# A linear recurrence over four batches of eight heads: steps of two batches by four heads, with halves swapped in the second batch

## The chip, the cores and the metric

The kernel runs on one core of a Trainium2 chip. The metric is the device time of one execution in microseconds. It is 399.98 us, the median of 3 runs (399.85 to 400.6).

Engine names are those of the profile: PE (matrix multiply) with PEld (its weight load), DVE (vector), ACT (scalar), POOL (GpSimd) and SP, which issues most DMAs.

## What is computed

A recurrence of the RWKV-5 kind over r, k and v (4 batches, 8 heads, 768 positions, 48 wide, float32), and then a mixture of experts over the 3072 resulting rows of 384:

```
state = zeros((B, H, D, D))
for t in range(S):
    cur = einsum('bhd,bhe->bhde', u * kt, vt)
    y[:, :, t] = einsum('bhd,bhde->bhe', rt, state + cur)
    state = w[:, :, None] * state + einsum('bhd,bhe->bhde', kt, vt)
x = y.transpose(0, 2, 1, 3).reshape(B * S, H * D)
...
# 4 groups x 4 experts; the best group and the best expert in it, a softmax weight of each
h = maximum(x[tokens of e] @ w1[e], 0)          # 384 -> 1024
out[tokens of e] = gate * (h @ w2[e])           # 1024 -> 384
```

## The kernel before

**The recurrence in steps.** Positions are taken 128 at a time. Within such a chunk the recurrence is written with matmuls: scores of keys against queries, masked to earlier positions; the masked scores times v; and the state of the chunks before times the queries. Powers of w are folded into tables: `pw` (multiplied into r when it is turned), `iw` (into the very first k) and `T2` (into the others). There are 24 steps. A step n is one chunk of one batch with all its 8 heads: group g = n // 2 has two batches, and half a = n % 2 picks one. The state of a batch comes back every fourth step (`R[n % 4]`).

**One step** (loop over s, line 860), as it stands on PE:

- `values(s)`: masked scores `am` times v, into bank YB, on two column halves of the array
- `update(s)`: k times v for the state, into bank MS
- `turn(far, ...)`: four transposes each of k (bank TR) and r (bank RW) for a later step
- `rows_out(s - 1)`: four transposes of the result into rows, bank YB
- `gate_sum` and `gate_parts`: the routing logits. gate_parts makes four partial products on four column strips of 32, into a bank of 128 columns, which ACT copies to `lT`; gate_sum adds the strips with the matrix `sel`
- `scores(s + 2)`: for each of four head pairs hc and each e, two matmuls (line 536), on the four quarters of the array: the pair's e picks the rows, and z, the half of the keys, the columns. Keys 0 to 63 meet 128 queries; keys 64 to 127 meet only the last 64, because the others come before them
- `state(s + 1)`: the state times the queries, into YB, on the same four quarters

Beside it DVE masks the scores into `am` (`mask`, line 543, a copy under the predicate `later`), carries the state (`carry`), multiplies `pw` into the turned r and runs the routing (route_1 to route_4). ACT copies results out of PSUM and writes the diagonals of `am` (`diagonal`, line 561; the r*u*k term). POOL multiplies r*k and that by u (`own`, lines 489 and 490), k by T2 (`scaled`, line 493), and scatters finished rows into x_sorted with indirect DMAs (line 230). Order on each engine is the order of the program. In steps 0 to 5 (CLOSE is 5) the scores of step s + 1 are made in step s, so that mask and values follow each other directly; from step 5 on they are made two steps ahead, and the masks one.

**Loads.** r, k and v come in tiles of 128 positions by 2 batches by 8 heads by 48. `load` issues one DMA per batch on SP (line 323). The first r and k are issued on SP and ACT in turn (line 344).

**Start.** POOL and DVE build the tables, PE turns r, k and iw; in between stand transposes whose results aren't used (`turn_nothing`). ACT fills the pads of the k and r tiles, copies u, then T2.

**The end of the recurrence and the experts.** The two largest experts get their first 128 tokens ahead (`up_ahead`, `down_ahead`). Then 16 experts follow in a fixed order; the last one's rows are made token by row (`rows_down`, line 238), multiplied by the gate on ACT (line 244) and scattered by POOL (line 245).

`out_of_range` (line 751) tells whether w lay outside the range that the tables allow; a matmul (line 756) makes its result common to all partitions in step 0.

## Time and profile before

| what | us |
|---|---|
| median of the runs | 399.98 |
| the profiled execution, whole | 402.09 |
| its span, first to last instruction | 400.3 |
| values of step 0, 1, 2, 3 start at | 12.14, 16.86, 20.95, 25.01 |
| values of step 4, 5, 6, 7 start at | 30.57, 37.91, 44.53, 49.53 |
| values of step 23 start at | 127.43 |
| first expert matmul after the recurrence (line 1104) | 152.16 |
| last matmul starts | 392.66 |
| last scatter by POOL starts | 394.03 |

| line | what | count | mean ns |
|---|---|---|---|
| 536 | PE, scores, 128 columns | 368 | 276 |
| 536 | PE, scores, 64 columns | 368 | 235 |
| 583 | PE, values | 384 | 277 |
| 543 | DVE, mask, 128x1024 | 24 | 1323 |
| 561 | ACT, diagonal, 128x128 | 152 | 398 |
| 493 | POOL, k times T2, 128x384 | 24 | 1006 |
| 624 | ACT, lT out of PSUM, 128x128 | 24 | 260 |

The durations of PE are those of single instructions in a pipeline: they overlap, and what a stage costs is read from where it starts and where the next one starts. float32 matmuls show as two instructions each.

### The profile page before, as it was taken

The numbers are of one execution on the slowest core, as the hardware profiler recorded it, in microseconds if no ns is written. First come the engines' busy times: TensorE is split into PE (matmuls) and PEld (weight loads), VectorE is DVE, ScalarE is ACT, GpSimd is POOL, SyncE is SP. The second block draws the span as 40 slices with busy tenths as digits, with TensorE's granted clock in tenths as the row PEclk, the third lists the DMA queues.
The fourth block names the chain that finished last, engine by engine and source line by source line (L and its number), as shares of the span: only waits on it lengthen the run. The fifth ranks groups of instructions, "written<-read, shape, count | busy, mean of one in ns | idle before, by whom it ended". The sixth has DMA issues, their size and how long they took to land.

```text
span 400.3 us, 10467 instructions
## 1 busy us (share of the span) xinstructions
PE 388.7 (97%) x3963; PEld 361.9 (90%) x3963; DVE 153.4 (38%) x405; ACT 180.4 (45%) x429; POOL 201.0 (50%) x265
## 2 busy tenths in 40 slices
PE   8999999999999999999999999999999999999992
PEld 6787899999888977899999999999999999999981
DVE  7887988888867602101202112111121221211110
ACT  4665888888875211432433424424244244244210
POOL 7999956999842412105162351532624524523542
PEclk9999999999999999999999999999999999999999
DMA  8998999995965977999999999999989999981000
GB/s 159 160 174 159 197 208 221 212 195 147 264 200 123 308 193 212 233 275 258 232 258 243 228 250 266 224 253 284 200 240 259 255 247 268 233 236 28 27 18 27
DMA packets 123118, 81.80 MB, mean 204 GB/s; under 512 B 96863, under 2 KB 114289, under 8 KB 123061
## 3 DMA queue, kind: packets, MB, share of 16 engines
q1 hardware_dynamic: 116019, 71.12, 77.1%
q0 software_dynamic: 4752, 9.55, 8.1%
q8 instruction: 32, 0.52, 0.6%
q10 hardware_dynamic: 2290, 0.40, 0.5%
q14 instruction: 25, 0.20, 0.2%
HBM read 69.89 MB, written 11.67 MB: 204 GB/s over the span
## 4 chain that ended last, share of the span: by engine, by line
issue 46%; PE 29%; POOL 18%; SPq 3%; DVE 2%; DMA 1%; POOLq 1%; ACT 0%
POOL out_dram L1128 16%; PE YB L583 6%; PE PA L536 6%; SPq L323 3%; PE TR L511 3%; PE YB L574 2%; PE YB L630 2%; PE RW L511 2%; PE MS L594 2%; PE TR L619 2%; PE MS L644 1%; DMA vt<-in_v_dram 1%; POOL out_dram L245 1%; PE TR L793 1%; DVE am L543 1%
## 5 line engine op out<-in xcount | busy, mean ns | idle before, releaser
L1128 POOL DMA_INDIRECT out_dram<-yt,idn x93 | 90.4, 972 | 137.1 <-DVE yt L1126 107.0
L1076 DVE STREAM_TRANSPOSE xe<-xg 128x672 f32<-128x672 f32 (+2 forms) x16 | 12.7, 796 | 121.0 <-DMA xg<-x_sorted 88.7
L1116 PE MATMUL YB<-hT,w2p 128*128 128x208 f32 (+10 forms) x336 | 58.7, 328 | 0.0
L1116 PE MATMUL PA<-hT,w2p 128*128 128x208 f32 (+10 forms) x336 | 58.1, 326 | 0.0
L1116 PEld LDWEIGHTS YB<-hT,w2p 128*128 128x128 f32 x336 | 55.8, 190 | 0.0
L1116 PEld LDWEIGHTS PA<-hT,w2p 128*128 128x128 f32 x336 | 55.3, 190 | 0.0
L561 ACT ACTIVATE am<-ident,du 128x128 f32<-128x128 f32 x152 | 50.5, 398 | 0.0
L1125 DVE STREAM_TRANSPOSE yt<-yT 128x672 f32<-128x672 f32 (+1 forms) x14 | 11.8, 842 | 80.4 <-ACT yT L1119 80.4
L1094 ACT COPY w2p<-w 128x1024 f32<-128x1024 f32 x42 | 41.1, 1045 | 3.0 <-DMA w<-in_moe_w_dram 3.0
L543 DVE COPY_PREDICATED am<-later,PA 128x1024 f32<-128x1024 int32 x24 | 31.7, 1323 | 10.8 <-PE PA L536 6.1
L1104 PE MATMUL MS<-xe,w 128*128 128x208 f32 (+12 forms) x192 | 32.8, 320 | 0.0
L1104 PE MATMUL TR<-xe,w 128*128 128x208 f32 (+12 forms) x192 | 32.8, 320 | 0.0
L1104 PE MATMUL RW<-xe,w 128*128 128x208 f32 (+12 forms) x192 | 32.8, 320 | 0.0
L1104 PE MATMUL SB<-xe,w 128*128 128x208 f32 (+12 forms) x192 | 32.7, 320 | 0.0
L1104 PEld LDWEIGHTS SB<-xe,w 128*128 128x128 f32 x192 | 30.8, 190 | 0.6 <-issue 0.2
L1104 PEld LDWEIGHTS MS<-xe,w 128*128 128x128 f32 x192 | 30.7, 190 | 0.0
L1104 PEld LDWEIGHTS RW<-xe,w 128*128 128x128 f32 x192 | 30.7, 190 | 0.0
L1104 PEld LDWEIGHTS TR<-xe,w 128*128 128x128 f32 x192 | 30.7, 190 | 0.0
L230 POOL DMA_INDIRECT x_sorted<-xt,place_i x16 | 16.1, 1003 | 23.6 <-DVE end L719 11.8
L536 PE MATMUL PA<-rT,kT 48*64 48x128 f32 (+1 forms) x736 | 25.6, 255 | 0.5 <-issue 0.5
L583 PE MATMUL YB<-am,vt 128*48 128x128 f32 x384 | 25.9, 277 | 0.1
L490 POOL TENSOR_TENSOR dg<-dg,ub 128x384 f32<-128x384 f32 x24 | 24.1, 1003 | 1.9
(220 smaller groups left out, 560.1 us busy)
## 6 DMA issues: line engine op xcount, KB each, us to landing
w<-in_moe_w_dram SPq DMA_DIRECT2D x128, 384.0 KB, 9.5
vt<-in_v_dram SPq DMA_DIRECT2D x24, 192.0 KB, 4.5
rp<-in_r_dram SPq DMA_DIRECT2D x23, 192.0 KB, 4.3
kt<-in_k_dram SPq DMA_DIRECT2D x22, 192.0 KB, 5.2
xg<-x_sorted SPq DMA_DIRECT2D x36, 85.8 KB, 10.3
x_sorted<-zeros SPq DMA_DIRECT2D x4, 392.0 KB, 4.7
out_dram<-yt,idn POOLq DMA_INDIRECT x93, 7.5
xg<-x_sorted SPq DMA_DIRECT2D x20, 73.5 KB, 8.9
```

The source lines that it names most:

```text
L230: ins = nc.gpsimd.indirect_dma_start(out=xs_dram, out_offset=bass.IndirectOffsetOnAxis(ap=place_i[:, i : i + 1], axis=0), in_=xt[:, i].rea ...
L490: nc.gpsimd.tensor_mul(dg, dg, ub)
L511: nc.tensor.transpose(ps[:, hc, :], two, ident)
L536: nc.tensor.matmul(PA[64 * z : 64 * (z + 1), e, P * hc + 64 * z : P * (hc + 1)], lhsT=kT[rows, hc, 64 * z : 64 * (z + 1)], rhs=rT[rows, hc ...
L543: nc.vector.copy_predicated(am[n % NAM], later.unsqueeze(1).unsqueeze(1).to_broadcast([P, 2, HC, P]).bitcast(I32), PA.rearrange("p e (h t) ...
L561: nc.scalar.mul(am[n % NAM][:, e, hc, :], ident, dus[n][:, i : i + 1])
L583: nc.tensor.matmul(y_at(e, hc), lhsT=vt[:, n % 2, 2 * hc + e, :], rhs=amn[:, e, hc, :], start=(n < 4 and hc < 2), stop=True, skip_group_ch ...
L1076: nc.vector.transpose(xe[:, :, 0:nb, :], xg[:, 0:nb, 0:QW].rearrange("p i (ko a) -> p ko i a", a=32))
L1094: nc.scalar.copy(o4[:, kk], v4[:, kk])
L1104: nc.tensor.matmul(ph[:, i, 0:n], lhsT=w1[:, ko, P * (f + i) : P * (f + i + 1)], rhs=xe[:, ko].rearrange("p i b -> p (i b)")[:, 0:n], star ...
L1116: nc.tensor.matmul(po[:, 0:n], lhsT=w2p[:, d, fo, :], rhs=hT[:, fo, 0:n], start=(fo == 0), stop=(fo == FO - 1))
L1128: ins = nc.gpsimd.indirect_dma_start(out=out_q, out_offset=bass.IndirectOffsetOnAxis(ap=idn[:, i : i + 1].bitcast(U32), axis=0), in_=yt[:, ...
```

## The change

A step is now one chunk of two batches with four heads each: step n takes heads 4 (n % 2) to 4 (n % 2) + 3 of both batches of its group. In the second batch of each pair the two halves of a chunk are swapped: partitions 0 to 63 hold positions 64 to 127 and the other way round. So the second batch loads with two DMAs of 64 partitions, its tables PW, IW and T2 are kept a second time with halves swapped, the mask has one triangle per head pair (LT), and token numbers (tok4) follow. In scores the long matmul of the second batch falls to the upper keys: quarters z = 0 and z = 1 exchange their lengths, and the pairs go in the order 0, 2, 1, 3.

gate_parts takes two steps at once (every second step), since a row of the result is now spread over two steps; it writes two blocks of TR, copied at once, and gate_sums has two matmuls. In steps before 5 these stand after the state. In step 4 the values are copied out after the diagonals, and one turn goes to bank PA. The range check moves to step 8 and shares the matmul of a count; fillers in the start go; `rows_of_table(1)` stands after the first scores, with `scaled(0, ...)` behind it. The last expert's rows are made and scattered in two halves of 192.

```diff
-    later = cst([P, P], "later")
+    LT = cst([P, HC, P], "LT")
+    later = LT[:, 0, :]
...
+    def half_down(hT, w2, i, n, z, po, yt):
+        cols = slice(DM // 2 * z, DM // 2 * (z + 1))
+        for fo in range(FO):
+            nc.tensor.matmul(
+                po[0:n, 0 : DM // 2], lhsT=hT[:, fo, 0:n], rhs=w2[:, fo, cols], start=(fo == 0), stop=(fo == FO - 1),
+                skip_group_check=True,
+            )
+        nc.scalar.mul(yt[0:n], po[0:n, 0 : DM // 2], tagA[i][0:n, 1:2])
+        ins = nc.gpsimd.indirect_dma_start(
...
-        def load_half(t, src, g, a, queue):
-            c, b = g // 2, 2 * (g % 2) + a
-            queue.dma_start(out=t[:, a], in_=src[b, :, P * c : P * (c + 1), :].rearrange("h t d -> t h d"))
+        def load_heads(t, src, g, queue, heads=slice(0, H)):
+            for b in range(2):
+                for rows, t0 in ((slice(0, P), 0),) if b == 0 else ((slice(0, 64), 64), (slice(64, P), 0)):
+                    t1 = P * (g // 2) + t0
+                    queue.dma_start(
+                        out=t[rows, b, heads],
+                        in_=src[2 * (g % 2) + b, heads, t1 : t1 + rows.stop - rows.start, :].rearrange("h t d -> t h d"),
+                    )
...
-        for a in range(2):
-            load_half(raw[0, "r"], r, 0, a, both[a])
-            load_half(raw[0, "k"], k, 0, a, both[1 - a])
+        for heads in (slice(0, 4), slice(4, 8)):
+            load_heads(raw[0, "r"], r, 0, nc.sync, heads)
+            load_heads(raw[0, "k"], k, 0, nc.scalar, heads)
...
+        PW = ring.tile([P, 2, HC, P], FP32, name="PW")
+        IW = am[3]
+        pw, iw = PW[:, 0], IW[:, 0]
...
-        turn_nothing(2)
         gates_in()
         pads(kp, 0)
         nc.scalar.copy(ub.rearrange("p h d -> p (h d)"), u_ps_all)
+        for t in (PW, IW):
+            for z in range(2):
+                nc.scalar.copy(t[:, 1, :, 64 * z : 64 * (z + 1)], t[:, 0, :, 64 * (1 - z) : 64 * (2 - z)])
+        for i in (1, 3):
+            nc.scalar.copy(LT[:, i, :], LT[:, i - 1, :])
...
+        def own(g, hf):
+            dg = dgs[2 * g + hf] = pool.tile([P, 2, 4, D], FP32, tag="dg", bufs=3, name="dg")
+            nc.gpsimd.tensor_mul(dg, four(raw[g, "r"], hf), four(raw[g, "k"], hf))
+            nc.gpsimd.tensor_mul(dg, dg, spread(ub[:, 4 * hf : 4 * hf + 4], 1, 2))
+
+        def scaled(g, hf):
+            nc.gpsimd.tensor_mul(four(kp[g % NKP], hf), four(raw[g, "k"], hf), four(T2, hf))
...
+        def columns_of(hc, z):
+            return (64 * z, P) if hc < 2 else (0, 64 * (z + 1))
 
         def scores(n):
             kT, rT = rkT.pop((n, "kT")), rkT[n, "rT"]
-            for hc in range(HC):
+            for hc in (0, 2, 1, 3):
                 for e in range(2):
                     rows = slice(DP * e, DP * e + D)
+                    for z in range(2):
+                        c0, c1 = columns_of(hc, z)
                         nc.tensor.matmul(
+                            PA[64 * z : 64 * (z + 1), e, P * hc + c0 : P * hc + c1],
+                            lhsT=kT[rows, hc, 64 * z : 64 * (z + 1)], rhs=rT[rows, hc, c0:c1],
                             start=True, stop=True, skip_group_check=True,
                         )
...
+        def part(n):
+            for b in range(2):
+                for e in range(2):
+                    q = 2 * (n % 2) + e
+                    nc.tensor.matmul(
+                        TR[32 * q : 32 * (q + 1), b, :], lhsT=gwp[:, 4 * (n % 2) + e, :], rhs=yTs[n][:, e, b, :],
+                        start=True, stop=True, skip_group_check=True,
+                    )
+
+        def gate_parts(n, first=True):
+            if first:
+                part(n - 1)
+            part(n)
+            mid[n] = pool.tile([P, 2, P], FP32, tag="lT", name="lT")
+            nc.scalar.copy(mid[n], TR[:, 0:2, :])
...
+        def rows_of_table(b, ps):
+            for hc in range(HC):
+                nc.tensor.transpose(ps[:, hc, :], IW[:, b, hc], ident)
+            nc.scalar.copy(
+                T2[:, b].rearrange("p (y e) d -> p y e d", e=2),
+                ps.rearrange("p y (e x) -> p y e x", x=DP)[:, :, :, 0:D],
+            )
...
+        rows_of_table(0, RW)
         own(0, 0)
-        scaled(0, 1)
         own(0, 1)
-        scaled(0, 0)
         sum_own(0)
         diagonal_here(0)
         diagonal(0, 1, HERE - HC)
         scores(0)
+        rows_of_table(1, whole_MS)
+        scaled(0, 1)
+        scaled(0, 0)
...
         mask(0)
-        turn_nothing(2)
         turn(1, "rT")
-        turn_nothing(4, TR)
         turn(1, "kT")
...
-            values_out(s)
+            if s != CLOSE - 1:
+                values_out(s)
             if s == 0:
                 own_term(1)
-                out_of_range()
             for n, e, hc in waiting:
                 diagonal(n, e, hc, hc + 1)
             waiting.clear()
+            if s == CLOSE - 1:
+                values_out(s)
...
             if s + 1 < NT:
                 state(s + 1)
+            if s < CLOSE:
+                if summed is not None:
+                    gate_sums(summed)
+                if parts is not None:
+                    gate_parts(parts)
             if s == CLOSE - 1:
-                turn(s + 3, "kT")
+                turn(s + 3, "kT", PA[:, 0].rearrange("p (h t) -> p h t", t=P))
...
+                if p == last:
+                    for z in range(2):
+                        yt = pool.tile([P, DM // 2], FP32, tag="yh", name="yh")
+                        half_down(hTs[p], held(p)[1], 2 + i, SLOTS[i], z, next_of(downs), yt)
```

## The prediction

> **What bounds the kernel now.** I read the page first (busy times and the row of slices), then busy time by stretches of 10 us, then the chain of waits and the timeline of the stages that the change touches.
>
> ```profile
> span 400.3 us, 10467 instructions
> PE 388.7 (97%) x3963; PEld 361.9 (90%) x3963; DVE 153.4 (38%) x405; ACT 180.4 (45%) x429; POOL 201.0 (50%) x265
> ```
>
> ```profile
> 50.00:60.00 10.00, 10.00 (x210) 9.03 (x208) 8.14 (x23) 8.06 (x26) 5.26 (x6) 1.00 0.95 208
> ...
> 70.00:80.00 10.00, 10.00 (x216) 9.06 (x214) 8.06 (x18) 8.05 (x26) 9.49 (x10) 1.00 0.97 212
> ```
>
> Columns: stretch, its length, busy time (and instructions) of PE, PEld, DVE, ACT, POOL, granted clock, DMA share, GB/s. PE is idle between 44 and 393 us only in two stalls of under 0.9 us near 103 and 110, so the experts (from 152 us) cost what their matmuls cost, and the change doesn't touch these. In the recurrence it decides what PE has to do per step. A regular step starts every 4.79 us (values at 59.73 and 64.52):
>
> ```profile
> 62.47 0.30 PE L644 MATMUL MS<-sel,lT 128*128 128x20 f32 x2
> 62.70 0.43 PE L619 MATMUL TR<-yT,gwp 128*32 128x128 f32 x8
> 63.05 0.99 PE L536 MATMUL PA<-rT,kT 48*64 48x128 f32 x30
> 63.78 0.31 PE L574 MATMUL YB<-rT,R 48*48 48x128 f32 x2
> 63.87 0.28 PE L536 MATMUL PA<-rT,kT 48*64 48x128 f32 x2
> 63.92 0.66 PE L574 MATMUL YB<-rT,R 48*48 48x128 f32 x14
> 64.52 0.75 PE L583 MATMUL YB<-am,vt 128*48 128x128 f32 x10
> ```
>
> Start, length, then the group. Two state matmuls (L574) start at 63.78, ahead of two scores matmuls (L536) at 63.87: one half of the array had run out of scores while the other had not. That imbalance is what the swapped halves remove.
>
> Before 44 us PE waits, and the steps are chains through several engines. The start, from the timeline:
>
> ```profile
> 2.43 0.60 ACTq L323 DMA_DIRECT2D rp<-in_r_dram  x1
> 3.06 1.28 ACT L349 ACT_TABLE_LOAD   x1 [3.06 <-DVE pw L380]
> 6.45 1.06 PE L511 MATMUL MS<-ident,rp 128*128 128x128 f32 x4
> 9.25 0.48 ACT L816 COPY T<-YB 128x384 f32<-128x384 f32 x1 [1.18 <-PE YB L815]
> 10.61 0.60 PE L511 MATMUL RW<-ident,rp 128*128 128x128 f32 x4
> 10.76 1.32 DVE L543 COPY_PREDICATED am<-later,PA 128x1024 f32<-128x1024 int32 x1
> 12.14 1.08 PE L583 MATMUL YB<-am,vt 128*48 128x128 f32 x16
> 16.86 1.08 PE L583 MATMUL YB<-am,vt 128*48 128x128 f32 x16
> ```
>
> and step 4 (30.57 to 37.91) from the chain:
>
> ```profile
> 33.13 1.33 DVE am L543
> 34.46 0.24 DVE ts L607
> ...
> 34.84 0.59 PE MS L644 x4
> 35.43 0.40 PE MS L619 x8
> 35.83 0.02 issue
> 35.85 0.27 ACT lT L624
> ```
>
> Mask, carry, logits, copy: DVE, PE and ACT wait in turn.
>
> **What the Trainium skill says.** "TensorEngine Tiling (Array Packing)", Key Properties: tiles load and multiply independently of each other, and a change of tiling mode drains the array. The trace agrees: see the overtaking above; PEld stands idle 0.20 us before the scores and 0.18 before the values, the two changes of mode. "TensorE: Matmul & The Clock Gate", Part 1: after an idle window of about 3.4 us the clock falls to half until a busy window has passed. The trace has only the first warming: four transposes take 1.06 us at 6.45 and 0.60 at 10.61. "DMA: Bandwidth & Descriptors", Anatomy of one DMA: a semaphore wait of a DMA is waited for by the issuing sequencer, with about 2 us fixed from issue to landing. Here ACT loads its table at 3.06, when its last issue ends; a 0.8 KB load took 2.0 us.
>
> **The change part by part.** The sum is made against the profiled execution (402.09 us, span 400.3); it is 2.1 us above the median of 399.98, and differences are carried over to the median unchanged.
>
> *Scores.* Sixteen matmuls in two passes, on four tiles. In the upper tiles a step has 8 passes of 128 columns, in the lower 8 of 64. From the timeline of single groups, passes of 128 follow at 0.109 us in a tile, and passes of 64 at 0.058. Before, the longer tiles take 8 x 0.109 = 0.872 (the chain has 0.92 for the group). After, each tile has 4 x 0.109 + 4 x 0.058 = 0.668. Gain 0.20 to 0.22 a step; the order 0, 2, 1, 3 keeps tiles at most one head apart, a lead that they have in the trace too. I take 0.215. It counts only where PE decides: in steps 6 to 21.
>
> *Gates.* gate_parts for two steps at once uses two column strips per step, four over both; 8 matmuls take 4 passes of 0.109 per strip = 0.44 in place of 0.22, if the second step's strips run beside the first's (if not, 0.7). A gate_sum is 0.22. Even steps: two sums in place of one sum and parts: 0.22 + 0.22 + the change of mode, 0.65, against 0.69 (62.36 to 63.05). Odd steps: parts alone, 0.22 more, and one sum 0.22 less: 0. So a pair of steps gains 2 x 0.215 + 0.04 = 0.47. Pairs 8/9 to 20/21: 7 x 0.47 = 3.3; step 6 gains 0.24; step 7 0.0 (two sums already). Steps 22 and 23 and the head of the tail lose 0.6: a second sum twice, and parts of one step on two strips only (0.22 more each), less one sum. Sum -2.95. The ACT copies (L624, 24 x 0.26) become 12 longer ones; cover: ACT is 0.8 busy. After the speed-up the next limits are POOL, at 4.25 us a step (three multiplies of 1.0 and one scatter) and DVE, 4.06; a PE step averages 4.55, so neither takes over.
>
> *Start.* DMAs: three per load in place of two, with the same bytes and packets; SP issues 25 of them ahead of the gate weights, not 15. In the compiled order a DMA waits for the one eight before it. The last three of ACT's eight loads so wait for the first pieces of r and k; with the first landings at 4.58 and 5.95 now for twice the bytes, I put that at about 4.9, so that ACT's table load starts near 5.4, not 3.06. ACT then also copies four half tables and two masks (4 x 0.31 + 2 x 0.2 = 1.6). T2's first half so comes at about 11.0 (9.73 now), the diagonals end at 12.0 (10.61), mask 0 at 13.3 (12.08). T2's second half ends at 12.4, POOL's scaled(0,1), now ahead of everything on POOL, at 13.4, turn(1,kT) on PE 14.0, and values(0) behind it 14.05 (12.14). Then values, values_out, diagonals, mask: 1.0 + 0.14 + 0.55 + 0.97 + 1.35 = 4.0, so values(1) at 18.05 (16.86; there 0.5 us went to the range matmul L756, which waited for the carry and goes). +1.2. Steps 1 and 2 have ACT's diagonals in this loop (4.06 and 4.09 us now), so shorter scores give nothing. POOL's three more fills and masks (some 0.3 us) lie beside the wait for the tables; its four iotas for one lie behind 1 us of lead.
>
> *Steps 3 to 5.* Step 3: the parts no longer wait for the carry ahead of the state (0.48 idle): -0.55. Step 4: diagonals ahead of values_out bring mask 5 0.7 forward, and the logits stand after the state with turn(7) in another bank; I add up PE alone: 1.0 + 0.75 + 0.5 + 0.6 + 0.95 + 0.7 + 0.5 + 0.7 + 0.95 = 6.6 against 7.34: -0.75. Step 5: the same DVE order up to the carry (4.3 after the start), then sums, scores, state: 6.15 against 6.62: -0.5. Front in all: 1.2 - 1.8 = -0.6.
>
> *Tail.* Last rows in two halves: PE the same 5.2 us, ACT 0.35 for 0.58, but POOL is held by the scatters of the expert before until 392.27 and then needs 1.28 per scatter: the second half issues at 393.9, not 394.03. -0.15. Masks, table multiplies and the memory fills keep their sizes (copy_predicated over 1024 elements 1.32): 0, on DVE with slack. The x_sorted chain after step 23 grows by 0.3; xe is ready 0.85 ahead of PE's need at 152.16, so 0.
>
> Sum: -0.6 - 2.95 - 0.15 = -3.7: span 396.6, median **396.3**.
>
> **Unknown costs.** The parts' overlap: 0 to +0.26 a pair, +2 at most; I take 0, since scores already show such a lead. ACT's wait for lanes: from 0 (table at 3.1, front 2 us better) to 2 us later. The scores' gain: 0 to 0.22. POOL multiplies on two blocks of four heads: rows of 48 out of 64 cost 1010 ns (L489) and contiguous ones 1003 (L490), so 0, at most 0.1 each, still hidden.
>
> **Rivals.** A, the scores don't shorten: 32 weight loads in 0.87 us are 27 ns each, and if loads came one after another, that would be the limit whatever the columns. For: the two numbers coincide. Against: loads of different tiles start 7 ns apart, and state overtakes scores. Time: the 3.4 us of scores gone, 399.7. B, the start is dearer: the idle stretch of PE from about 10.5 to 13.4, with the filler transposes gone, lets the clock fall for one window. Then steps 0 and 1 lose some 2.6 us: 398.9. C, slower: the same fall of the clock, lasting. At half clock the 3.2 us of PE work of a step become 6.4, more than the 4.05 of the loop, 2.3 us a step; because PE is busy only part of these steps the clock may not return. It decides from 3.7 / 2.3, about two steps; with three, 403. Against it: each step has over 3 us of matmuls. That the recurrence is not split as told can be excluded from the compiled order.
>
> **How the numbers follow.** Forecast 0.68 (its own range 394.6 to 397.8), A 0.06, B 0.19, C 0.07. Faster: forecast, B and a part of A, 0.88; within 0.2% (0.8 us, about what this measurement can tell) 0.05, from A; slower 0.07, C. Range 394.3 to 399.0: it holds B's centre and leaves out C, most of A and the edges.
>
> **What would show it.** Values of step 6 near 43.9 (44.53); regular steps alternating near 4.5 and 4.6; no state matmul ahead of a scores matmul; ACT's table load near 5.4; the clock row below 9 early would show B or C. If the step period stays 4.79 the scores' reasoning is wrong; if step 6 starts after 46, the front's.

## The result, and the profile after

The change made the kernel slower: 406.93 us (median of 6 runs, 404.64 to 409.24) against 400.29 for the kernel before in the same series (399.53 to 401.6), a ratio of 1.0158 with an interval of 1.0132 to 1.0184. The profiled execution takes 406.95 us, its span is 405.2, against 402.09 and 400.3 before. The forecast was 396.3 and faster. Some executions of a kernel fall into a slower state, with a lower granted clock; the ratios and intervals below, and the times that are set side by side, leave them out.

The page of the kernel after: its span, the busy times, and the row of granted clocks.

```profile
span 405.2 us, 10586 instructions
PE 386.5 (95%) x3989; PEld 362.1 (89%) x3989; DVE 154.1 (38%) x412; ACT 181.2 (45%) x425; POOL 203.4 (50%) x273
...
PEclk9699999999999999999999999999999999999999
```

PE is busy for 2.2 us less than before (388.7), so its work did shrink; the span grew by 4.9 all the same. The loss is idle time of PE, and the 6 near the left end of the last row (PEclk, tenths of full clock in 40 slices) says that its clock fell once. Laid end to end:

| stretch of the span | before | after | difference | forecast |
|---|---|---|---|---|
| start to values of step 0 | 12.14 | 15.20 | +3.1 | +1.9 |
| step 0 to 1 | 4.72 | 5.09 | +0.4 | -0.7 |
| step 1 to 6 | 27.60 | 27.06 | -0.5 | -1.8 |
| step 6 to 23 | 82.90 | 82.53 | -0.4 | -2.95 with the next row |
| step 23 to the first expert | 24.80 | 25.97 | +1.2 | |
| first expert to the start of the last matmul | 240.50 | 243.67 | +3.2 | 0 |
| from there to the end | 7.64 | 5.68 | -2.0 | -0.15 |

All starts are from the timelines: the values of step 6 at 47.35 (before 44.46; the 44.53 given above is the chain's piece, which begins a little later), of step 23 at 129.88 (127.36), the first expert at 155.85 (152.16).

First, what the change was for. The timeline of PE in a regular step of the kernel after (start, length, group):

```profile
64.84 0.66 PE L673 MATMUL TR<-yT,gwp 128*32 128x128 f32 x16
65.43 0.90 PE L588 MATMUL PA<-rT,kT 48*64 48x128 f32 x32
66.14 0.62 PE L626 MATMUL YB<-rT,R 48*48 48x128 f32 x16
66.69 0.75 PE L638 MATMUL YB<-am,vt 128*48 128x128 f32 x10
```

From the start of the scores (L588) to that of the state (L626) it is 0.71 us, where before it was 0.87 (63.05 to 63.92); no state matmul stands ahead of a scores matmul any more. Undisturbed pairs of steps take 4.46 + 4.68 = 9.14 us, against 9.56. The mechanism of the scores is there, with the forecast size.

Busy time by stretches shows where it goes: the columns are length, PE, PEld, DVE, ACT, POOL, clock, DMA share, GB/s.

```profile
50.00:60.00 10.00, 10.00 (x225) 8.89 (x224) 8.28 (x23) 8.34 (x26) 9.38 (x32) 1.00 0.86 182
...
70.00:80.00 10.00, 8.57 (x199) 7.59 (x199) 7.10 (x17) 6.92 (x21) 9.28 (x10) 1.00 0.93 187
...
200.00:210.00 10.00, 8.89 (x51) 8.57 (x50) 2.91 (x6) 3.79 (x7) 4.46 (x5) 1.00 0.97 257
```

From 70 to 80 PE was full before, and the DMAs moved 212 GB/s; now PE is idle for 1.43 us there, and they move 187. The same from 50 to 60: 182 for 208 GB/s. The timeline names the two stalls in the recurrence (in brackets the idle time and what ended it):

```profile
44.26 0.66 PE L565 MATMUL TR<-ident,kp 128*128 128x128 f32 x4 [1.81 <-POOL kp L538]
...
74.50 0.66 PE L565 MATMUL TR<-ident,kp 128*128 128x128 f32 x4 [1.43 <-POOL kp L538]
```

PE waits for POOL's `kp`, that is for `scaled`. POOL itself is not too slow. Its own timeline:

```profile
34.29 1.01 POOL L534 TENSOR_TENSOR dg<-rp,kt 128x384 f32<-128x384 f32 x1 [3.69 <-DMA rp<-in_r_dram]
...
70.16 1.20 POOL L232 DMA_INDIRECT x_sorted<-xt,place_i  x1 [8.09 <-ACT am L613]
...
73.45 1.00 POOL L538 TENSOR_TENSOR kp<-kt,T 128x384 f32<-128x384 f32 x1
```

At 34.29 POOL has stood idle for 3.69 us until r landed; the work behind it is late by that, and reaches PE at 44.26. Before, at this place, POOL ran without a gap (groups at 32.14, 33.23, 34.55). The second stall has another carrier: POOL is held for 8.09 us ahead of its first scatter of rows into `x_sorted`. The profile puts that down to ACT, but what fits is a DMA: the last of the four fills of `x_sorted` with zeros has to land first (fill_early below tests this). The chain of waits of the kernel after has its issue:

```profile
64.30 0.74 SPq L348
...
65.08 0.65 SPq L480
```

L480 is that fill. An estimate: from 65.08, a landing of 5.3 us (the median of the three fills issued between 20 and 60 us) gives 70.4, and the scatter starts at 70.16. Before, it went out at 57.60, and the timeline of POOL before has

```profile
63.07 1.20 POOL L230 DMA_INDIRECT x_sorted<-xt,place_i  x1 [7.65 <-DVE ohg L178]
```

So the fill is 7.5 us later, though the step in which it belongs is later by only 2.6: SP's queue is behind.

The start, from the timeline of the kernel after:

```profile
6.08 1.28 ACT L376 ACT_TABLE_LOAD   x1 [6.08 <-DMA rp<-in_k_dram]
8.95 0.69 DVE L576 TENSOR_TENSOR rT<-MS,PW 128x512 f32<-128x512 f32 x1 [1.54 <-ACT PW L468]
11.29 0.47 ACT L881 COPY T<-RW 128x384 f32<-128x384 f32 x1
13.09 1.98 POOL L538 TENSOR_TENSOR kp<-rp,T 128x384 f32<-128x384 f32 x2 [1.67 <-ACT T L881]
14.15 1.12 PE L565 MATMUL TR<-ident,kp 128*128 128x128 f32 x4 [1.58 <-POOL kp L538]
15.20 1.95 PE L638 MATMUL YB<-am,vt 128*48 128x128 f32 x16
17.08 1.56 PE L588 MATMUL PA<-rT,kT 48*64 48x128 f32 x32
```

The table load comes at 6.08 (3.06 before), and DVE's first product then waits 1.54 us more for the swapped copy of `PW`, since step 0 now holds both batches. PE has idle gaps of 1.50 us ahead of the first scores at 10.29 and of 1.58 ahead of 14.15. The values take 1.95 us in place of 1.08: the granted clock is 0.50 from 14 to 18 us (it falls between 12.2 and 12.4).

In the experts the page of the kernel after shows, for the issue of the gathers of expert rows (count, KB each, us from issue to landing):

```profile
xg<-x_sorted SPq DMA_DIRECT2D x36, 85.8 KB, 12.6
```

It was 10.3 before. The waits of the kernel after from 125 us on have PE itself waiting for such rows (us in total, number of times, longest):

```profile
PE SB L1187 <- DVE xe L1159: 2.4, 2, 1.3
```

Before, there was no such wait; DVE's `xe` waited for the gathers for 88.7 us in all, now for 149.4.

### The profile page after: what moved, and what is told of

Its sections match the earlier page's. It is cut to its first block, busy times and chain, and to the rows that moved or that the text cites. A ratio compares the mean times of both kernels' runs of the same rounds, so it can differ in the third digit from the quotient of the medians.

```text
span 405.2 us, 10586 instructions
## 1 busy us (share of the span) xinstructions
PE 386.5 (95%) x3989; PEld 362.1 (89%) x3989; DVE 154.1 (38%) x412; ACT 181.2 (45%) x425; POOL 203.4 (50%) x273
## 4 chain that ended last, share of the span: by engine, by line
issue 47%; PE 24%; POOL 20%; DMA 2%; ACT 2%; SPq 2%; DVE 1%; POOLq 1%; ACTq 0%
POOL out_dram L1211 16%; PE YB L638 5%; PE PA L588 4%; PE TR L565 3%; PE YB L626 2%; PE YB L689 2%; PE RW L565 2%; SPq L348 2%; PE TR L673 2%; PE MS L649 2%; DMA kt<-in_k_dram 1%; PE MS L706 1%; DMA rp<-in_k_dram 1%; POOL kp L538 1%; POOL out_dram L247 1%
## 5 line engine op out<-in xcount | busy, mean ns | idle before, releaser
L1159 DVE STREAM_TRANSPOSE xe<-xg 128x672 f32<-128x672 f32 (+2 forms) x16 | 12.7, 797 | 149.4 <-DMA xg<-x_sorted 149.4
L613 ACT ACTIVATE am<-ident,du 128x128 f32<-128x128 f32 x152 | 49.6, 397 | 0.0
L595 DVE COPY_PREDICATED am<-LT,PA 128x1024 f32<-128x1024 int32 x24 | 32.4, 1349 | 9.9 <-ACT am L613 5.1
L1208 DVE STREAM_TRANSPOSE yt<-yT 128x672 f32<-128x672 f32 (+1 forms) x14 | 11.8, 842 | 55.4 <-ACT yT L1202 55.4
L638 PE MATMUL YB<-am,vt 128*48 128x128 f32 x384 | 27.1, 283 | 0.8 <-ACT kT L574 0.5
L638 PEld LDWEIGHTS YB<-am,vt 128*48 128x48 f32 x384 | 20.7, 126 | 5.6 <-issue 4.0
## 6 DMA issues: line engine op xcount, KB each, us to landing
xg<-x_sorted SPq DMA_DIRECT2D x36, 85.8 KB, 12.6
```

The lines of the kernel that those rows point to most:

```text
L595: nc.vector.copy_predicated(am[n % NAM].rearrange("p e h t -> p e (h t)"), spread(LT.rearrange("p h t -> p (h t)"), 1, 2).bitcast(I32), PA,)
L613: nc.scalar.mul(am[n % NAM][:, e, hc, :], ident, dus[n][:, i : i + 1])
L638: nc.tensor.matmul(y_at(e, hc), lhsT=vt[:, *head(n, e, hc), :], rhs=amn[:, e, hc, :], start=(n < 4 and hc < 2), stop=True, skip_group_chec ...
L1159: nc.vector.transpose(xe[:, :, 0:nb, :], xg[:, 0:nb, 0:QW].rearrange("p i (ko a) -> p ko i a", a=32))
```

## The experiments

Theory Q (the queue of loads): the loss comes from the third DMA per load, which puts SP behind, and with it r, the fill and the first data of the experts. Rivals: the start alone does it, by the clock (F) or by the way the first loads are split (S); or the recurrence in two batches by four heads is itself slower, whatever the loads (L in the first two expectations). Later expectations add R: the swapped halves and the shorter scores ask more of POOL, DVE or memory than they give. Each kernel is timed beside the kernel before in the same series.

The first four kernels below (the two without the swap, and the two of the start) ran in a series in which the kernel before took 400.74 us (399.55 to 402.26); all later ones in series in which it took 414 to 424. There the intervals of the ratios are 1.5 to 3 per cent wide, so that those ratios decide little, and every profile shows 1.1 to 4.3 us of stalls of PE between 105 and 130 us that the trace puts down to PE's own issue (0.6 before, 1.9 after the change); the kernel before has no profile from these series. So of the later runs only ratios with their intervals, and the places of stalls before 100 us, are used.

### Without the swap, with two and with three DMAs per load

Both kernels keep everything but the swapped halves: the tables of the second batch are plain copies and all long scores fall to the same quarters, as before. They differ from each other in one line, which the first r and k share.

```diff
# no_swap
-for rows, t0 in ((slice(0, P), 0),) if b == 0 else ((slice(0, 64), 64), (slice(64, P), 0)):
+for rows, t0 in ((slice(0, P), 0),):
...
-base=NQ * (S * b + 64 * (z ^ b)), channel_multiplier=NQ,
+base=NQ * (S * b + 64 * z), channel_multiplier=NQ,
...
-return (64 * z, P) if hc < 2 else (0, 64 * (z + 1))
+return (64 * z, P)
# no_swap_3dma, against no_swap
-for rows, t0 in ((slice(0, P), 0),):
+for rows, t0 in ((slice(0, P), 0),) if b == 0 else ((slice(0, 64), 0), (slice(64, P), 64)):
```

> The changed kernel without the swapped halves: the second batch loads with one DMA (two per load, as before), its tables and mask are plain, and the long matmul of a scores pair is in the same quarter for all pairs. Theory Q (the third DMA of each load makes SP's queue late; POOL and then PE wait for r and for the last memory fill): SP issues the r of step 1 and the fill of step 8 early again, POOL does not wait near 30 us, the two PE stalls ahead of turned k (1.9 us near 44, 1.5 us near 74) are gone, and step 6 starts about 2 us earlier than in the changed kernel (45.3 against 47.35); the regular step is about 0.2 us longer (about 4.75). Rival L (the two-batch layout itself makes POOL and PE late, whatever the loads): both stalls stay and step 6 starts within 0.5 us of 47.35.

> As no_swap, but the second batch is loaded with two DMAs of 64 rows, so that each load has three DMAs as in the changed kernel, with the same bytes and packets. Only the number of DMAs differs from no_swap. Theory Q: the stalls near 44 and 74 us are back, step 6 starts 2 us later than in no_swap and step 23 3 to 4 us later. Rival L: no difference from no_swap above 0.5 us at step 6.

| | no_swap | no_swap_3dma |
|---|---|---|
| time, median | 401.35 (400.26 to 404.49, 12 runs) | 406.95 (403.55 to 408.79, 4 runs) |
| ratio to before | 1.0021 (1.0000 to 1.0042) | 1.0125 (1.0073 to 1.0176) |
| values of steps 6, 12, 23 | 46.11, 76.25, 127.51 | 46.96, 78.67, 130.79 |
| first expert, last matmul | 152.79, 393.49 | 160.63, 401.33 |

Two DMAs of half the size in place of one, with the same bytes, cost 5.6 us by the medians and 4.2 by the ratios (1.0125 - 1.0021, of 400.74); the two intervals don't meet. Its signs are those of the kernel after. The timeline of PE with three DMAs (with two, neither stall is there in this series):

```profile
43.68 0.66 PE L563 MATMUL TR<-ident,kp 128*128 128x128 f32 x4 [1.24 <-POOL kp L536]
...
75.16 0.66 PE L563 MATMUL TR<-ident,kp 128*128 128x128 f32 x4 [1.50 <-POOL kp L536]
...
143.25 1.09 PE L858 MATMUL PA<-xeA,w 128*128 128x128 f32 x5 [2.57 <-DMA w<-in_moe_w_dram]
```

The third line is later in the same queue: weights of an expert. Of the 7.84 us by which the first expert is later with three DMAs, 0.85 are there at step 6 (2 were expected) and 3.28 at step 23 (3 to 4), and the other 4.56 arise at this wait and the matmuls behind it. The queue of SP with two and with three DMAs shows when the second set of weights is issued:

```profile
126.90 1.82 SPq L137 DMA_DIRECT2D w<-in_moe_w_dram  x3
```

```profile
133.74 2.52 SPq L137 DMA_DIRECT2D w<-in_moe_w_dram  x3
```

Before it was 123.87, and after the change 131.18. Why SP falls behind, from the DMAs in 20 to 60 us (count, KB each, us to landing), first with two per load, then with three:

```profile
DMA packets 33362, 7.13 MB, mean 178 GB/s; under 512 B 32585, under 2 KB 33353, under 8 KB 33353
...
kt<-in_k_dram SPq DMA_DIRECT2D x10, 192.0 KB, 5.3
```

```profile
DMA packets 29454, 6.35 MB, mean 159 GB/s; under 512 B 28688, under 2 KB 29444, under 8 KB 29444
...
kt<-in_k_dram SPq DMA_DIRECT2D x5, 192.0 KB, 5.5
kt<-in_k_dram SPq DMA_DIRECT2D x10, 96.0 KB, 4.4
```

A DMA of 64 rows moves half the bytes and takes 4.4 us, not half of 5.5; for r and v the halves take 4.4 and 4.1 us, and the whole ones 3.9 and 4.1. Two readings of why SP falls behind stand side by side, and no run parts them. The first is an estimate of what is under way: in a program where a DMA waits for the one eight before it, eight DMAs of this mix hold 8 x (192 + 96 + 96) / 3 = 1024 KB, where eight whole ones hold 1536 KB, which goes in the direction of the 159 for 178 GB/s. The second is SP's own time: by its timeline it issues the two DMAs of a load in 1.10 us (at 21.81 in no_swap) and three in 1.80 (at 22.97 in no_swap_3dma); over the 17 loads from 14 to 66 us this is an estimated 12 us more. The reserve that goes is to be seen in the waits of SP for other engines, in which it is ahead of the work, from 14 to 66 us: 12.9 us in all before, 12.3 with two DMAs, 7.5 with three, 6.1 in the kernel after. The Trainium skill, "DMA: Bandwidth & Descriptors", Rules for kernel authors, says of "Two transfers to disjoint partition halves": "Don't bother — they serialize", and advises one transfer of 128 partitions. This pair agrees with the advice, with the 4.2 to 5.6 us beside it; that the halves serialize, no run here shows.

Without the swap the scores do not gain either. PE in a regular step of no_swap:

```profile
64.78 0.99 PE L586 MATMUL PA<-rT,kT 48*64 48x128 f32 x30
65.50 0.31 PE L624 MATMUL YB<-rT,R 48*48 48x128 f32 x2
65.59 0.28 PE L586 MATMUL PA<-rT,kT 48*64 48x128 f32 x2
```

The overtaking is back, and a pair takes 4.65 + 4.88 = 9.53. Against 9.14 this makes the swap worth 0.19 to 0.20 us a step, measured by itself (forecast 0.215). So the swap brings what it should per step, about 3 us over steps 6 to 21, and its loads cost more. In the whole time even these 3 us are not to be seen: with three DMAs the ratio is 1.0158 with the swap and 1.0125 without it. And the split of the recurrence without the swap is within 0.4% of the kernel before in this series, which leaves the last rival at most 0.4 of the 1.6%.

### The start: clock and first loads

```diff
# fillers
 rows_of_table(0, RW)
+turn_nothing(12, YB[:, :, 0:P])
...
 turn(1, "rT")
+turn_nothing(12, YB[:, :, 0:P])
 turn(1, "kT")
# first_loads_3
-for heads in (slice(0, 4), slice(4, 8)):
-    load_heads(raw[0, "r"], r, 0, nc.sync, heads)
-    load_heads(raw[0, "k"], k, 0, nc.scalar, heads)
+load_heads(raw[0, "r"], r, 0, nc.sync)
+load_heads(raw[0, "k"], k, 0, nc.scalar)
```

> The changed kernel with 12 transposes whose results are not used behind the first rows_of_table and 12 between turn(1, rT) and turn(1, kT), where PE was idle for 1.5 and 1.6 us. Theory (the idle PE drops the granted clock for one window): the clock stays at 1.0 from 10 to 20 us, values of step 0 take 1.08 us in place of 1.95 and scores 0.9 in place of 1.56, and values of step 1 start 1.4 us earlier (18.9 against 20.29) with values of step 0 unchanged. Rival: the clock was not limiting, since mask 1 and POOL decide step 1: values of step 1 start within 0.4 us of 20.29.

> The changed kernel with the first r and k loaded in three DMAs each (all eight heads at once) in place of six. Theory: ACT's table load at 6.08 us waits for the issue of its six DMAs; with three it comes at about 4.0, the copies on ACT follow 2 us earlier, and values of step 0 start at about 13.5 (15.20). Rival: the landing of the first r and k sets the start (all eight heads now land together and late), and values of step 0 stay within 0.4 us of 15.2 or come later.

The timeline of PE in fillers:

```profile
14.81 1.08 PE L638 MATMUL YB<-am,vt 128*48 128x128 f32 x16
...
18.88 1.08 PE L638 MATMUL YB<-am,vt 128*48 128x128 f32 x16 [0.63 <-DVE am L595]
```

With PE kept busy the clock stays at 1.00, the values take 1.08 us, and step 1 starts at 18.88 for 20.29: the clock's fall had cost 1.41 us. But the time is 407.29 (406.85 to 412.17), ratio 1.0151 (1.0130 to 1.0173): nothing of it is to be seen. POOL's timeline (of the slowest of the six runs, 412.17 us) says why:

```profile
35.53 1.01 POOL L534 TENSOR_TENSOR dg<-rp,kt 128x384 f32<-128x384 f32 x1 [3.96 <-DMA rp<-in_r_dram]
```

An earlier start meets the same late r, and step 6 starts at 48.58. In first_loads_3 ACT issues three DMAs for six ahead of its table load, which comes at 3.87 as expected (expected 4.0). Values of step 0 start at 14.78 only (expected 13.5), because POOL's `scaled` waits for the second half of T2:

```profile
3.87 1.28 ACT L375 ACT_TABLE_LOAD   x1 [3.87 <-DVE wcol L417]
...
13.13 1.97 POOL L537 TENSOR_TENSOR kp<-rp,T 128x384 f32<-128x384 f32 x2 [0.60 <-ACT T L880]
```

Step 1 starts at 18.84; then stalls of 1.97 us at 43.7 and 2.33 at 74.8. The times are 404.43 and 406.33 (2 runs), which give no interval. So F and S are real as events, and neither explains the whole: in these profiles the start gives back 1.4 us, and the recurrence takes it again while its loads are late. no_swap says the same from the other side. It has the late and slow start too, as PE's timeline shows:

```profile
14.51 1.95 PE L636 MATMUL YB<-am,vt 128*48 128x128 f32 x16
19.66 1.08 PE L636 MATMUL YB<-am,vt 128*48 128x128 f32 x16
```

Its step 1 is 2.80 us behind the kernel before, and by step 23 (127.51 for 127.36) it has made that up.

### Moving the fill

```diff
-if s in (5, 6, 7, 8):
+if s in (5, 6, 7):
     fill(s - 5)
+if s == 7:
+    fill(3)
```

> The changed kernel with one memory fill (the fourth, of x_sorted) issued on SP in step 7, ahead of the loads of step 8, in place of behind them. Theory Q2: POOL's first scatter waits for this fill, POOL's products for later steps stand behind the scatter, and PE's stall of 1.4 us near 74 is the end of that chain; with the fill about 9 us earlier the first scatter starts at 63 to 65 us (70.16), the stall near 74 is gone and step 12 starts about 1.5 us earlier relative to step 6 (29.0 us behind it in place of 30.5). The stall near 44 stays. Rival: the scatter waits for the routing on DVE, which the change delays; then it stays near 70 and the stall stays.

POOL's timeline:

```profile
63.52 1.20 POOL L232 DMA_INDIRECT x_sorted<-xt,place_i  x1 [1.45 <-ACT am L613]
...
67.25 1.01 POOL L534 TENSOR_TENSOR dg<-rp,kt 128x384 f32<-128x384 f32 x1 [2.53 <-DMA rp<-in_r_dram]
```

The scatter starts at 63.52 for 70.16 (71.15 in the changed kernel in a later series, changed_again below). This shows that the fill, not ACT, held POOL. The stall of PE near 74 is gone (that step takes 4.76 us for 6.19), and steps 6 to 12 take 29.57 for 30.47 (expected 29.0); but changed_again, whose step 11 starts only at 75.53 for 72.17 here, has no stall there either, so for the stall the pair is not clean. The stall near 44 stays, with 1.95, as it must if that one is r's. Then r is late by 2.53 at 67.25, and the ratio is 1.0142 (1.0068 to 1.0216): the queue is behind, and another of its loads takes the place of the fill.

### Fewer DMAs with the swap kept

If the number of DMAs is the matter, loads can be merged: two groups of batches in one DMA, three DMAs for two loads in place of six. Of the edit, the new load:

```diff
+nc.sync.dma_start(
+    out=t[rows, b].rearrange("p g h d -> p (g h) d"),
+    in_=src[2 * b : 2 * b + 2, :, t1 : t1 + rows.stop - rows.start, :].rearrange("g h t d -> t (g h) d"),
+)
```

merged does this from the first v and the second chunk on; merged_first3 has the first r and k in three DMAs each, too; late_merge has these as well, merges only from the fourth chunk on (the loads of the earlier ones still come apart) and loads the gate weights later; late_merge_2 has in addition the early fill. changed_again is the changed kernel in the series of late_merge.

> The changed kernel with swapped halves, but a group holds batches g and g + 2, so that batches 0 and 1 are plain and 2 and 3 swapped, and from chunk 1 on one load serves two groups: three DMAs for four steps and each of r, k, v in place of six (nine for four steps in place of 18; before had 12), same bytes and packets. Theory Q (number of DMAs): POOL does not wait for r near 30 us, no PE stall above 0.7 us near 44 and 74, step 6 near 45, regular steps 4.46 and 4.68 as in the changed kernel, step 23 at about 126.5 (129.88), no wait of PE for rows in the experts above 0.5 us, median about 399. Rival R (swapped halves and shorter scores ask more of POOL, DVE or memory than they give, however loaded): the stalls stay and the median is above 404.

> As merged, with the first r and k in three DMAs each in place of six. In the changed kernel alone this brought values of step 1 from 20.29 to 18.84 us but no time, which theory Q puts down to the loads behind. Theory Q: with few loads the 1.4 us now last to the end, step 6 is 1 to 1.5 us earlier than in merged and the median about 1 us lower. Rival: the front is set by POOL's order or by the landing of the second group, and step 6 differs by less than 0.4 us.

> The changed kernel unaltered, as the yardstick for the three runs beside it. Median 405 to 409 us where the kernel before takes about 400; the stalls of PE near 44 and 74 us are there again, of 1 to 2.5 us each.

> The changed kernel with fewer DMAs on SP: first r and k in three each, the gate weights behind the loads of step 0, and from chunk 3 on one load serves two groups (batches 0 and 1 plain, 2 and 3 swapped), so three DMAs for four steps and each of r, k, v in place of six. Theory Q: values of step 1 near 18.9 us, r of the third group is issued about 4 us earlier than in the changed kernel, the PE stalls near 44 and 74 us fall below 0.7 us, regular steps stay 4.46 and 4.68, step 23 starts near 126 (before 127.4, changed 129.9), median 397 to 400, so below the kernel before. Rival R (swapped halves and shorter scores ask more of POOL, DVE or memory than they give, however loaded): stalls stay and the median is within 2 us of changed_again.

> late_merge with the fourth fill in step 7 as in fill_early. Theory Q: no PE stall above 0.7 us between 20 and 100 us, regular steps 4.46 and 4.68, step 23 at 125 to 127 us where memory is as fast as in the first runs; median below the kernel before beside it by 1 to 3 us. Rival R (swapped halves and shorter scores ask more of memory or POOL than they give, however loaded): other stalls take their place and the median is not below the kernel before.

| | ratio to before | what it shows |
|---|---|---|
| merged | 1.0351 (1.0202 to 1.0500) | stalls 1.78 at 36.8 (v), 2.14 at 50.4 |
| merged_first3 | 1.0368 (1.0229 to 1.0506) | step 6 at 55.10 |
| changed_again | 1.0189 (1.0060 to 1.0318) | stall 1.98 at 45.0, as in the first profile; none near 74 |
| late_merge | 1.0104 (0.9963 to 1.0245) | stall at 44.7 only 0.43, but 5.13 at 78.1 |
| late_merge_2 | 1.0258 (1.0180 to 1.0337) | stalls 1.37 at 33.5, 3.41 at 85.7 |

None of them brought what was expected. A merged load brings the second group's data, needed two steps later, together with the first's, so that what is needed now can come later: in merged a DMA for r takes 7.09 us. In late_merge the stall at 44 nearly went, but the fill went behind the merged loads, and POOL's first scatter with it:

```profile
73.75 1.20 POOL L232 DMA_INDIRECT x_sorted<-xt,place_i  x1 [9.60 <-ACT yT L683]
```

late_merge_2 ends that, and then POOL waits 3.03 us for r at 58.46. The number of DMAs is thus not all. That the order of the data is the rest fits these traces, but no run tests it alone. And by the tests set for them the merges came out on the side of R: other stalls took the place of the old ones, and no ratio came out below 1. No run has the swapped halves with loads that are on time, so R is not excluded.

### The start without doubled tables

no_swap_start loads the first r and k as the kernel before does, leaves out the second copies of the tables, which no_swap doesn't need, and puts `scaled(0, ...)` and four filler transposes back where they stood; no_swap_start_2 is the same kernel again.

```diff
-for heads in (slice(0, 4), slice(4, 8)):
-    load_heads(raw[0, "r"], r, 0, nc.sync, heads)
-    load_heads(raw[0, "k"], k, 0, nc.scalar, heads)
+for b in range(2):
+    for key, src, queue in (("r", r, both[b]), ("k", k, both[1 - b])):
+        queue.dma_start(out=raw[0, key][:, b], in_=src[b, :, 0:P, :].rearrange("h t d -> t h d"))
...
-for t in (PW, IW):
-    for z in range(2):
-        nc.scalar.copy(t[:, 1, :, 64 * z : 64 * (z + 1)], t[:, 0, :, 64 * z : 64 * (z + 1)])
```

> no_swap with the start of the kernel before: first r and k in two DMAs each on SP and ACT in turn, no second tables (the plain ones are spread over both batches), scaled(0, ...) back among own(0, ...), four filler transposes before turn(1, kT). Theory (the start's loss is ACT's issues and table copies and the later scaled): values of step 0 at about 12.3 us (14.51), step 6 about 2.2 us earlier (43.9), median about 2 us below no_swap (399.3). Rival (loads set the front even with two DMAs each): step 6 stays within 0.5 us of 46.1.

> no_swap_start once more, since its first run fell on a chip where the kernel before took 420 us. Theory: values of step 0 at about 12.3 us, step 6 at about 44, median 398.5 to 400 where the kernel before takes about 400 and no_swap 401.4. Rival (loads set the front even with two DMAs each): step 6 within 0.5 us of 46.1 and median above 401.

Values of step 0 start at 15.84 and 14.80 (expected 12.3), and step 6 at 47.11 and 45.33 (expected 44). PE's timeline of no_swap_start has the reason:

```profile
8.77 0.69 PE L560 MATMUL MS<-ident,rp 128*128 128x128 f32 x2 [2.11 <-DMA rp<-in_r_dram]
```

PE waits 2.11 us for r of the second batch. Step 0 with two batches by four heads needs all four first loads where step 0 with one batch needed two; with whole loads that seems to cost as much as the tables did (values at 14.51 in no_swap). The ratios are 1.0164 (1.0035 to 1.0293) and 1.0111 (1.0003 to 1.0219).

### The tail

The last expert's rows in one piece, as before, in no_swap; a repeat of it.

```diff
-for z in range(2):
-    yt = pool.tile([P, DM // 2], FP32, tag="yh", name="yh")
-    half_down(hTs[p], held(p)[1], 2 + i, SLOTS[i], z, next_of(downs), yt)
+yt = pool.tile([P, DM], FP32, tag="yd", bufs=1, name="yd")
+rows_down(hTs[p], held(p)[1], 2 + i, SLOTS[i], next_of(downs), yt)
```

> no_swap with the last expert's rows made and scattered whole (one scatter of 384) in place of two halves of 192. Reading of the two traces: from the last matmul to the end 7.6 us as before in place of 5.7, because the last scatter's rows take 5.3 us to land in place of 3.7; median about 1.9 us above no_swap (403.2). Forecast's working: 0.15 us, no difference that can be measured.

> no_swap_whole_tail once more for the same reason. If the smaller last scatter is what shortened the end, the stretch from the last matmul to the end of the span is 7.6 us again (no_swap 5.4) and the median 1.9 us above no_swap's 401.4. If the 7.6 us of the kernel before was chance, it is 5.5 to 6 us, and the median is 401.4 to 402.

The ratio of the first is 1.0135 (0.9980 to 1.0290), which decides nothing; the repeat has no interval. From the start of the last matmul to the end it is 5.7 us in both, and 5.9 in before_3dma below, which has whole rows too. With halves it was 5.3 to 5.7 in the first series, but 6.5 to 7.6 in all nine profiles of the later ones: there the scatters of the halves wait up to 2.1 us (in changed_again 1.28 and 1.26). So within the later series the halves look dearer by 0.6 to 1.9 us, and the 7.6 us that the kernel before took with whole rows in its one profile is not what whole rows always take. What the halves are worth stays open.

### A third DMA in the kernel before

```diff
-for a in range(2):
-    load_half(t, src, g, a, nc.sync)
+load_half(t, src, g, 0, nc.sync)
+c, b = g // 2, 2 * (g % 2) + 1
+for z in range(2):
+    t1 = P * c + 64 * z
+    nc.sync.dma_start(
+        out=t[64 * z : 64 * (z + 1), 1], in_=src[b, :, t1 : t1 + 64, :].rearrange("h t d -> t h d")
+    )
```

no_swap_again ran beside it.

> The kernel before, with one edit: from the second load on, the second batch of each load comes in two DMAs of 64 rows in place of one of 128 (three DMAs per load, same bytes and packets). Theory Q (number of DMAs): SP loses its slack, PE stalls appear ahead of turned k or of the carry between steps 3 and 12, step 12 starts at least 2 us later than 74.56, and the time is 1.0 to 1.8 per cent above the kernel before. Rival: three DMAs hurt only the changed step with its earlier needs; then less than 0.3 per cent and step 12 within 0.7 us of 74.56.

> no_swap unaltered, beside before_3dma on the same chip. Theory Q: ratio to the kernel before 0.998 to 1.006 (1.0021 in its first run), clearly below before_3dma; no PE stall above 0.7 us between 20 and 100 us. Rival: above 1.01.

The ratios are 1.0168 (1.0034 to 1.0301) and 1.0139 (0.9991 to 1.0286; below 1.006 was expected). In before_3dma the waits of SP fall from 12.9 to 2.6 us, so the reserve goes here too; but up to step 11 no step is late, and step 12 only by 0.9 measured from the start of step 0 (expected at least 2). The kernel before takes one batch with eight heads and needs half of a group's load at first, so that it can stand a late second half longer: an explanation that was not tried. In this series no_swap, level with the kernel before in the first, has nearly the ratio of before_3dma, so the two cannot be told apart there. That a third DMA costs the kernel before anything is not shown.

no_swap_again has more to say. With two DMAs per load, PE's timeline has the stall that was taken for the mark of the third:

```profile
42.20 0.66 PE L563 MATMUL TR<-ident,kp 128*128 128x128 f32 x4 [1.78 <-POOL kp L536]
```

So have the two kernels of the tail (1.78 us each). What goes with this stall is how long POOL had waited for r ahead of it: 0.98 to 1.47 us in the three profiles with two DMAs that have no stall (no_swap and the two of no_swap_start), 1.95 to 2.77 in the three that have it, 3.04 with three DMAs in no_swap_3dma and 3.69 in the kernel after. (before_3dma, one batch with eight heads to a step, takes 4.04 us of it with a stall of 0.40.) By these traces it is late loads that make the stall; the third DMA is one thing that goes with late loads, and in the later series they are late without it too.

No version was shown to beat the kernel before.

## Why the prediction was wrong

**The step that failed** is this one: "DMAs: three per load in place of two, with the same bytes and packets; SP issues 25 of them ahead of the gate weights, not 15." It was priced only where ACT's table load waits for its lanes, and at nothing after the start. The pair no_swap and no_swap_3dma measures the missing term in one series: +4.2 us by the ratios, +5.6 by the medians (406.95 - 401.35). It is paid in pieces, none of which is on SP: PE waits for POOL at 44 and 74, and weights and expert rows come later. The view that could have given warning was the DMA share, 0.95 and 0.97 in the very windows quoted: the forecast shows these numbers and draws nothing from them. How a third DMA makes the queue late (bytes under way, or SP's time for each issue) stays open.

**"the experts (from 152 us) cost what their matmuls cost, and the change doesn't touch these."** They took 3.2 us more, 2.4 of it PE's two waits for rows. From 160 us to 280 the DMA share was 1.01 to 1.10 before and 1.00 to 1.02 after, so there is little reserve in which a late queue could catch up. That they inherited the delay is read from the profile (weights issued 7.3 us later, gathers landing in 12.6 for 10.3 us) and not shown by a run: in no_swap_3dma, where those weights are issued later still (133.74), the experts took 240.70, as in no_swap. There the delay was paid ahead of them (first expert +7.84).

**Front: -0.6 forecast, +2.9 measured at step 6.** Step 1 was forecast +1.2 and came +3.43. Of the 2.2 that were missing, 1.41 is the clock (fillers), and about 0.8 is left for the longer chain: DVE waits for the swapped `PW`, and the table load comes at 6.08 rather than 5.4. Steps 3 and 4 gave -0.52 and -0.80 for -0.55 and -0.75: right. Step 5 gave +0.68 for -0.5: the stall at 44.26. "If step 6 starts after 46, the front's" was the test for a wrong front, and it spoke rightly.

**Rival B, the clock,** came true as an event, though the gap ahead of the fall is that from 8.8 to 10.3 us, not the forecast's idle stretch of 10.5 to 13.4, and at 1.41 us for the 2.6 that it was priced at: by 19.2 us the clock was full again, so that step 1 ran at full pace. As a cause of the result it falls: without it (fillers) the ratio is the same. C asked for a lasting half clock; the clock is 1.00 from 20 us on. A asked that scores not shorten; they did. None of the rivals held a late SP queue. C alone had the kernel slower, with a chance of 0.07, and the slowing that came is not C's.

**Scores and gates: right.** A pair of steps gained 0.42 for 0.47, and the swap alone 0.19 to 0.20 a step for 0.215. Over steps 6 to 23 only 0.4 us arrived. With the stalls taken out, the pairs 8/9 to 18/19 gained 0.34 to 0.59 each and 6/7 gained 0.29; pair 20/21 gained nothing, and step 22 lost 0.39, which makes 2.6 in all. Against it stand the stall of 1.43 at 74.5 and 0.8 more of stalls that the trace puts down to PE's own issue (1.58 at 112.4 and 0.33 at 118.5; before, 0.50 and 0.64 near 103 and 110; their cause is open).

**After step 23: "xe is ready 0.85 ahead of PE's need at 152.16, so 0".** It took 1.2 us more. 0.48 of it are the sums and parts of the last steps, which the forecast counted among its 0.6; no_swap has them too (25.28 us for 24.80). The other 0.69 stand at 140.09, where the trace has PE wait 0.54 us for a copy of ACT's, not for xe; no_swap has no such wait. Why the copy came late is open.

**Tail: -0.15 forecast, -2.0 in the profile.** From the start of the last matmul to the last scatter it was 1.37 (392.66 to 394.03) and is 1.06 (399.52 to 400.58): -0.3. The rest, 1.65, stands behind the last scatter: 6.27 us to the end before, 4.62 after. before_3dma has the old tail and 4.5 us there, so this part is no property of the halves; that it made the loss smaller is chance.

## What to carry to other kernels

Count the DMAs of a change, not only their bytes: a load cut in two halves of 64 rows kept its latency (k: 4.4 for 5.5 us) and took 4 to 6 us in the one pair that measures it, more than the 3 us of the balanced matmuls that it served. Where the DMA share is above 0.9, look for what else stands in the same queue (a fill, the next stage's weights), and follow it to whoever waits for that, even if PE is full at the moment. A gain on PE counts only as far as the loads can follow. Merging loads did not help here. And repeat the pair that carries the argument: the stall that told its two kernels apart in one series stood in the better one, too, in the next.

## What was not expected of the hardware

The clock fell to 0.50 without a long pause. By windows of 0.2 us it fell between 12.2 and 12.4 us, with PE at work, and was back between 19.0 and 19.2. Ahead of the fall PE had one gap of 1.50 us, up to 10.29; from 8.8 to 12.2 it was busy for 1.87 us of 3.40. In fillers it was busy for 3.20 of the same 3.40, and the clock stayed at 1.00. The gap of 1.58 us ahead of 14.15 came after the fall. The Trainium skill, "TensorE: Matmul & The Clock Gate", Part 1, has the clock fall after at least one idle window of about 3.4 us; a threshold for a partly busy window it does not give, and these profiles show one stretch that did not keep the clock and one that did. changed_again fell in the same way, between 11.8 and 12.0 us, with a gap of 2.95 us up to 11.02. The clock column doesn't show every slow stretch: in no_swap it reads 1.00 from 14 to 18 us, and the values of step 0 take 1.95 us there all the same.

A DMA share above 1.00 in windows of 40 us (1.10 before, 1.09 in no_swap) stands beside 245 to 255 GB/s in the experts, and 0.9 to 1.0 beside 162 to 184 GB/s in the recurrence, whose rows are of 192 bytes. From 20 to 60 us nearly all packets are under 512 B (31848 of 32711 before), from 160 to 280 us fewer than half (8560 of 20652). So the share says how full the queues are, not what they move; that the size of the pieces makes the difference fits these numbers.
